# A fused convolution and MLP kernel: a reworked prologue (w1 centred by 32-row matmuls, one load queue, idle matmuls) and fewer, larger token groups

## The chip, the cores and the metric

The kernel runs on 1 core of one Trainium2 chip. The metric is device time in microseconds (us) of the whole program; lower is better. Faster or slower needs 2%.

The engines have their names from the profile: PE multiplies matrices (PEld is its weight load), DVE, ACT and POOL work on vectors, SP issues DMA transfers. The granted clock is the share of its full clock that PE had by the profile; "half clock" means that it reads 0.50.

## The reference, cut to what matters

```python
# x: (8, 4224, 192) f32, weight: (8 heads, 7 taps)
w = softmax(weight)                                   # over the taps
y[b, s, h, :] = sum_k w[h, k] * x_padded[b, s + k, h, :]   # causal, 24 channels a head
# then, on y:
xn = (y - mean) / sqrt(var + 1e-6) * g_ln
out = y + relu(xn @ w_ch1) @ w_ch2                    # w_ch1 192x768, w_ch2 768x192, both given as float64
```

## The kernel before

Each of the 128 partitions holds 33 consecutive tokens of a sequence. A group is n tokens of each partition, 128 n tokens in all. For every group DVE convolves (7 taps x 8 heads = 56 instructions), transposes in 32x32 blocks and takes statistics; PE multiplies by w1 in 32-row tiles ("up"), ACT applies the ReLU, PE multiplies by w2 with the full array ("down"), DVE scales and adds. The mean is not subtracted from the tokens: w1 is centred instead, once, in the prologue. The weights arrive as float64 and are unpacked by integer and float instructions on DVE and ACT. Up, in before:

```python
for f in range(NF):                       # 6 slices of 128 hidden channels
    ph = [psum.tile([P, 512], F32, tag="ps") for q in range(NQ)]      # 4 of the 8 banks
    for c in range(NC):                   # 6 x 32 input channels
        for q in range(NQ):               # 4 row tiles, concurrent: a "quad"
            rows = slice(C * q, C * q + C)
            nc.tensor.matmul(ph[q][:, 0 : n * C], w1[rows, c, fs], t[rows, 0:n, c, :], ...)
    for q in range(NQ):
        nc.scalar.activation(ht[g][:, f, 0:n, q, :], ph[q]..., AF.Relu)
```

Down takes a bank for two tokens, from the same eight; DVE's add frees it. The order in which the engines get their work:

```python
first_tap(0); conv(0); centre_w1(); first_tap(1); transpose(0)
# unpack w2
for g in range(NG):
    load_x(g + 2)
    if g == 0: conv(1)
    up(g)
    if g > 0: first_tap(g + 1); conv(g + 1)
    transpose(g + 1)
    stats(g)
    down(g)            # matmuls on PE, then the adds on DVE, then the store
```

So on DVE the adds of group g come after the convolution, the transpose and the statistics that stand ahead of them.

## Time and profile before

| | before |
|---|---|
| median of its first 3 runs (range) | 1081.69 us (1080.77 to 1082.42) |
| profiled span | 1080.5 us |
| PE starts group 0 | 37.7 us |
| one group of 11 tokens on PE | 43.2 us |
| sequence 0 on PE (7, 8, 9, 9 tokens) | 132.0 us, of it about 2 waiting |

PE is busy from 37.7 us to the last microseconds. The work behind that cannot shrink, so read the table as: what comes ahead of 37.7, what PE loses between pieces of work, and where it waits. The lines themselves stand in the prediction.

### The profile page before, as it was taken

The numbers are of one execution on the slowest core, as the hardware profiler recorded it, in microseconds if no ns is written. First come the engines' busy times: TensorE is split into PE (matmuls) and PEld (weight loads), VectorE is DVE, ScalarE is ACT, GpSimd is POOL, SyncE is SP. The second block draws the span as 40 slices with busy tenths as digits, with TensorE's granted clock in tenths as the row PEclk, the third lists the DMA queues.
The fourth block names the chain that finished last, engine by engine and source line by source line (L and its number), as shares of the span: only waits on it lengthen the run. The fifth ranks groups of instructions, "written<-read, shape, count | busy, mean of one in ns | idle before, by whom it ended". The sixth has DMA issues, their size and how long they took to land.

```text
span 1080.5 us, 24335 instructions
## 1 busy us (share of the span) xinstructions
PE 1057.4 (98%) x10512; PEld 898.8 (83%) x10512; DVE 822.2 (76%) x2363; ACT 240.3 (22%) x636; POOL 16.9 (2%) x23
## 2 busy tenths in 40 slices
PE   3999999999999999999999999999999999999998
PEld 3999987978978879789788797897887978978878
DVE  5999798696696876966968769669687696696821
ACT  3521122031131220311312203113122031131220
POOL 3000000000000000000000000000000000000000
PEclk9999999999999999999999999999999999999999
DMA  8022022022022020230220302203202022020011
GB/s 241 2 82 89 4 96 96 30 75 103 2 103 89 16 104 31 74 103 1 104 102 3 103 31 74 104 1 103 102 2 103 32 73 104 1 104 41 2 42 41
DMA packets 9195, 70.55 MB, mean 65 GB/s; under 512 B 1280, under 2 KB 2304, under 8 KB 3329
## 3 DMA queue, kind: packets, MB, share of 16 engines
q1 hardware_dynamic: 8768, 68.02, 18.3%
q8 instruction: 82, 1.34, 0.5%
q10 hardware_dynamic: 224, 0.98, 0.4%
q14 instruction: 25, 0.20, 0.1%
q0 software_dynamic: 96, 0.00, 0.0%
HBM read 43.05 MB, written 25.95 MB: 64 GB/s over the span
## 4 chain that ended last, share of the span: by engine, by line
PE 96%; DVE 2%; DMA 1%; issue 0%; ACT 0%; ACTq 0%; DVEq 0%
PE po L352 48%; PE ph L329 48%; DVE y L265 1%; DMA raw<-in_moe_w_ch_dram 1%; DVE yt L273 0%; DVE w1f L184 0%; DVE scale1a L174 0%; ACT scale1b L166 0%; DVE scale1b L174 0%; DVE power1a L163 0%; DVE mant1a L157 0%; DVE power1a L159 0%; DVE y L357 0%; ACTq L130 0%; DVE power1b L163 0%
## 5 line engine op out<-in xcount | busy, mean ns | idle before, releaser
L352 PEld LDWEIGHTS po<-w,ht 128*128 128x128 f32 x3168 | 513.5, 190 | 13.3 <-issue 11.7
L352 PE MATMUL po<-w,ht 128*128 128x192 f32 x3168 | 522.5, 327 | 0.0
L329 PE MATMUL ph<-yt,w 32*128 32x352 f32 (+3 forms) x7200 | 520.4, 444 | 1.0 <-DVE yt L273 1.0
L329 PEld LDWEIGHTS ph<-yt,w 32*128 32x128 f32 x7200 | 367.4, 185 | 146.1 <-issue 5.4
L265 DVE SCALAR_TENSOR_TENSOR y<-xg,taps,y 128x264 f32<-128x264 f32 (+3 forms) x1200 | 473.7, 474 | 0.0
L334 ACT ACTIVATE ht<-ph 128x352 f32<-128x352 f32 (+3 forms) x600 | 222.7, 459 | 792.3 <-PE ph L329 792.3
L357 DVE SCALAR_TENSOR_TENSOR y<-po,r,y 128x192 f32<-128x192 f32 x264 | 96.5, 412 | 228.0 <-PE po L352 225.3
L286 DVE BATCH_NORM_STATS2 st<-y 128x6 f32<-128x192 f32 x264 | 70.1, 341 | 0.0
L273 DVE STREAM_TRANSPOSE yt<-y 128x2112 f32<-128x2112 f32 (+3 forms) x25 | 57.3, 2290 | 0.9
L257 DVE TENSOR_SCALAR y<-xg,taps 128x264 f32<-128x264 f32 (+1 forms) x184 | 51.4, 351 | 0.0
L237 PE MATMUL pw<-w1f,centre 128*128 128x128 f32 x144 | 18.0, 292 | 18.7 <-DVE w1f L184 18.7
L237 PEld LDWEIGHTS pw<-w1f,centre 128*128 128x128 f32 x144 | 17.9, 208 | 18.6 <-issue 18.6
L101 POOL MEMSET xg<- 1x1152 f32 x8 | 8.4, 1048 | 779.6 <-DVE y L265 779.6
L312 DVE SCALAR_TENSOR_TENSOR r<-d,r 128x11 f32<-128x11 f32 (+3 forms) x75 | 12.7, 170 | 2.6
L308 DVE TENSOR_TENSOR d<-r 128x11 f32<-128x11 f32 (+3 forms) x75 | 12.7, 170 | 2.6
L309 DVE SCALAR_TENSOR_TENSOR d<-d,v 128x11 f32<-128x11 f32 (+3 forms) x75 | 12.7, 170 | 2.6
L240 ACT COPY w<-pw 128x512 f32<-128x512 f32 (+1 forms) x12 | 5.7, 477 | 8.8 <-PE pw L237 8.6
L255 ACT ACTIVATE y<-xg,taps 128x168 f32<-128x168 f32 (+1 forms) x16 | 5.6, 432 | 0.0
L157 DVE TENSOR_SCALAR mant1a<-raw 128x768 uint32<-128x768 uint32 x1 | 0.6, 559 | 6.0 <-DMA raw<-in_moe_w_ch_dram 6.0
L289 DVE TENSOR_TENSOR d<-st 128x11 f32<-128x11 f32 (+3 forms) x25 | 4.4, 177 | 0.9
L300 DVE TENSOR_SCALAR d<-v 128x11 uint32<-128x11 uint32 (+3 forms) x25 | 4.3, 173 | 0.9
L297 DVE TENSOR_SCALAR v<-v 128x11 f32<-128x11 f32 (+3 forms) x25 | 4.3, 173 | 0.9
(46 smaller groups left out, 47.4 us busy)
## 6 DMA issues: line engine op xcount, KB each, us to landing
xg<-in_x_dram SPq DMA_DIRECT2D x14, 1632.0 KB, 9.2
out_dram<-y SPq DMA_DIRECT2D x20, 1056.0 KB, 4.9
xg<-in_x_dram SPq DMA_DIRECT2D x7, 1428.0 KB, 10.8
xg<-in_x_dram SPq DMA_DIRECT2D x2, 1440.0 KB, 12.5
out_dram<-y SPq DMA_DIRECT2D x2, 864.0 KB, 4.4
xg<-in_x_dram SPq DMA_DIRECT2D x1, 1344.0 KB, 14.1
xg<-in_x_dram SPq DMA_DIRECT2D x7, 191.2 KB
raw<-in_moe_w_ch_dram SPq DMA_DIRECT2D x1, 1152.0 KB
```

The costliest lines, as they stand in the source:

```text
L237: nc.tensor.matmul(dst, m[:, c, :], w1f[:, s, o : o + P], start=start, stop=not start)
L257: nc.vector.tensor_scalar(out=dst, in0=src, scalar1=tap, scalar2=None, op0=ALU.mult)
L265: nc.vector.scalar_tensor_tensor(out=y[g][:, 0:n, cs], in0=t[:, k : k + n, cs], scalar=taps[:, h, k : k + 1], in1=y[g][:, 0:n, cs], op0=AL ...
L273: nc.vector.transpose(yt[g][:, 0:n].rearrange("p j c t -> p (j c t)"), y[g][:, 0:n].rearrange("p j d -> p (j d)"),)
L286: nc.vector.bn_stats(out=st[:, j, :], in_=y[g][:, j, :])
L308: nc.vector.tensor_tensor(d, r, r, op=ALU.mult)
L309: nc.vector.scalar_tensor_tensor(out=d, in0=d, scalar=-0.5, in1=v, op0=ALU.mult, op1=ALU.mult)
L312: nc.vector.scalar_tensor_tensor(out=r, in0=d, scalar=1.5, in1=r, op0=ALU.add, op1=ALU.mult)
L329: nc.tensor.matmul(ph[q][:, 0 : n * C], w1[rows, c, fs], t[rows, 0:n, c, :], start=(c == 0), stop=(c == NC - 1),)
L334: nc.scalar.activation(ht[g][:, f, 0:n, q, :], ph[q][:, 0 : n * C].rearrange("p (j t) -> p j t", t=C), AF.Relu,)
L352: nc.tensor.matmul(dst, t[:, f, j, :, :].rearrange("p q t -> p (q t)"), w2[:, f, :], start=(f == 0), stop=(f == NF - 1),)
L357: nc.vector.scalar_tensor_tensor(out=yg[:, j, :], in0=dst, scalar=rstd[g][:, j : j + 1], in1=yg[:, j, :], op0=ALU.mult, op1=ALU.add,)
```

## The change

The intent: let PE start sooner (w1's bytes first, w1 unpacked in an order that needs less of it at once, centring by a copy and a subtraction of the mean in 32-row tiles, a first group of 6 tokens), keep PE's clock up until it starts (24 idle matmuls), and have fewer group borders (16 and 17 tokens a group in place of 11, each up in two halves so that a matmul still fits a bank). The setup tensors share the room of the later hidden tile, and x has two buffers in place of three. The loads of x0 (the tokens of group 0) are cut differently too, their padding apart from the tokens; that part is not in this core of the diff:

```diff
-        sizes = [J] * (R // J) + [R % J] * (R % J > 0)
-        if b == 0:
-            rest = R - 15
-            sizes = [7, 8, rest // 2, rest - rest // 2]
+        for n in (6, 8, 10, R - 24) if b == 0 else (J - 1, J):      # J = 17, R = 33
 ...
-    xpool = ctx.enter_context(tc.tile_pool(name="xin", bufs=3))
+    xpool = ctx.enter_context(tc.tile_pool(name="xin", bufs=2))
 ...
-    nc.gpsimd.dma_start(out=ga, in_=g_col[0:P, :])
+    nc.scalar.dma_start(out=ga, in_=g_col[0:P, :])
 ...
-    nc.scalar.dma_start(
-        out=raw1[:, 1:3].rearrange("p s f w -> p (s f w)"), in_=w1_words[0:P, :]
+    nc.sync.dma_start(
+        out=raw1[:, 0:2].rearrange("p s f w -> p (s f w)"), in_=w1_words[0:P, :]
     )
     for r in range(2):
-        (nc.sync, nc.scalar)[r].dma_start(
-            out=raw1[Q * r : Q * r + Q, 0, :, :].rearrange("p f w -> p (f w)"),
+        nc.sync.dma_start(
+            out=raw1[Q * r : Q * r + Q, 2, :, :].rearrange("p f w -> p (f w)"),
 ...
     def centre_w1():
-        (72 products of 128x128 with centre = 1 - 1/D, 12 copies)
+        for r in range(2):                          # the means, on all partitions
+            nc.tensor.matmul(pm[:, 0:FH], share[0], w1f[:, r, :], start=True, stop=False)
+            nc.tensor.matmul(pm[:, 0:FH], share[1 + r], w1f[:, 2, :], start=False, stop=True)
+            nc.scalar.copy(mean[:, FH * r : FH * r + FH], pm[:, 0:FH])
+        for s, parts in (...):                      # copy 32 rows to 128, take the mean off
+            ... nc.tensor.matmul(pw[q][:, 0:FH], copy[rows], w1f[rows, s, :], ...)
+            ... nc.tensor.matmul(pw[q][:, 0:FH], less[rows], mean[rows, ...], ...)
+            ... nc.scalar.copy(w1[:, c, FH * r : FH * r + FH], pw[q][:, 0:FH])
+    def keep_warm(times):
+        idle = psum.tile([P, 512], F32, tag="ps", name="idle")
+        for _ in range(times):
+            nc.tensor.matmul(idle[:, 0:P], less, copy, start=True, stop=True)
 ...
+        half = n if n <= 11 else (n + 1) // 2
         for f in range(NF):
+            for i0 in range(0, n, half):            # a block: 6 quads into 4 banks
 ...
     centre_w1()
+    keep_warm(24)
     first_tap(1)
```

Note the third index of raw1: in before slot 0 holds the two 192 KB transfers with the last 64 rows of w1 and slots 1 and 2 the 768 KB transfer; in the changed kernel the 768 KB come first.

More of the change, by code (lines that the diff above doesn't have):

```diff
@@ L51 @@
     R = S // P
-    J = 11
+    J = 17
     NF = F // P
@@ L56 @@
     FH = F // 2
-    assert D == P + Q and S % P == 0 and J * C <= 512 and NF % 2 == 0
+    assert D == P + Q and S % P == 0 and R % 2 and R // 2 + 1 == J and NF % 2 == 0
     groups = []
     for b in range(B):
-        sizes = [J] * (R // J) + [R % J] * (R % J > 0)
-        if b == 0:
-            rest = R - 15
-            sizes = [7, 8, rest // 2, rest - rest // 2]
         j0 = 0
-        for n in sizes:
+        for n in (6, 8, 10, R - 24) if b == 0 else (J - 1, J):
             groups.append((b, j0, n))
             j0 += n
-        assert j0 == R and max(sizes) <= J
+        assert j0 == R
+    assert max(n for _, _, n in groups) <= J
     NG = len(groups)
@@ L100, in load_x @@
             return
+        if b:
+            nc.sync.dma_start(
+                out=flat[:, 0 : (PAD + n) * D],
+                in_=bass.AP(
+                    tensor=x.tensor, offset=(b * S - PAD) * D, ap=[[R * D, P], [1, (PAD + n) * D]]
+                ),
+            )
+            nc.gpsimd.memset(t[0:1, 0:PAD, :], 0.0)
+            return
         nc.gpsimd.memset(t[0:1, 0:PAD, :], 0.0)
+        nc.sync.dma_start(out=flat[:, PAD * D : (PAD + n) * D], in_=xr[b, :, 0 : n * D])
         for p0, p1 in ((16, P), (1, 16)):
             nc.sync.dma_start(
-                out=flat[p0:p1, 0 : (PAD + n) * D],
-                in_=bass.AP(
-                    tensor=x.tensor, offset=(b * S + p0 * R - PAD) * D,
-                    ap=[[R * D, p1 - p0], [1, (PAD + n) * D]],
-                ),
+                out=flat[p0:p1, 0 : PAD * D],
+                in_=xr[b, p0 - 1 : p1 - 1, (R - PAD) * D : R * D],
             )
-        nc.sync.dma_start(out=flat[0:1, PAD * D : (PAD + n) * D], in_=xr[b, 0:1, 0 : n * D])
     taps = consts.tile([P, H, K], F32, name="taps")
@@ L117, with carve @@
     gb = consts.tile([P, 1], F32, name="gb")
-    raw1 = setup.tile([P, 3, FH, 2], U32, name="raw1")
+    room = hpool.tile([P, NF * J * P], F32, tag="ht", name="room")
+    taken = [0]
+    def carve(n, dtype):
+        part = room[:, taken[0] : taken[0] + n].bitcast(dtype)
+        taken[0] += n
+        return part
+    raw1 = carve(6 * FH, U32).rearrange("p (s f w) -> p s f w", f=FH, w=2)
     raw2 = setup.tile([P, NF * D, 2], U32, name="raw2")
@@ L122 @@
     g_col = moe_g_ln.rearrange("(d o) -> d o", o=1)
-    nc.gpsimd.dma_start(out=ga, in_=g_col[0:P, :])
+    nc.scalar.dma_start(out=ga, in_=g_col[0:P, :])
     for r in range(2):
-        nc.gpsimd.dma_start(out=gb[Q * r : Q * r + Q, :], in_=g_col[P:D, :])
+        nc.scalar.dma_start(out=gb[Q * r : Q * r + Q, :], in_=g_col[P:D, :])
     nc.sync.dma_start(
@@ L129 @@
     )
-    nc.scalar.dma_start(
-        out=raw1[:, 1:3].rearrange("p s f w -> p (s f w)"), in_=w1_words[0:P, :]
+    nc.sync.dma_start(
+        out=raw1[:, 0:2].rearrange("p s f w -> p (s f w)"), in_=w1_words[0:P, :]
     )
     for r in range(2):
-        (nc.sync, nc.scalar)[r].dma_start(
-            out=raw1[Q * r : Q * r + Q, 0, :, :].rearrange("p f w -> p (f w)"),
+        nc.sync.dma_start(
+            out=raw1[Q * r : Q * r + Q, 2, :, :].rearrange("p f w -> p (f w)"),
             in_=w1_words[P:D, 2 * FH * r : 2 * FH * (r + 1)],
@@ L148, with split_words @@
     nc.vector.memset(low, -896.0 * (1 << 23))
-    def split_words(raw, name):
-        n = raw.shape[1]
+    def split_words(raw, mant, power):
         hi = raw[:, :, 1]
-        mant = setup.tile([P, n], I32, name="mant" + name)
-        power = setup.tile([P, n], I32, name="power" + name)
-        high = setup.tile([P, n], F32, name="high" + name)
-        scale = setup.tile([P, n], I32, name="scale" + name)
         nc.vector.tensor_single_scalar(mant.bitcast(U32), hi, 0xFFFFF, op=ALU.bitwise_and)
-        nc.scalar.activation(high, mant, AF.Relu, scale=2.0**-20, bias=1.0)
+        nc.scalar.activation(mant.bitcast(F32), mant, AF.Relu, scale=2.0**-20, bias=1.0)
         nc.vector.tensor_scalar(
@@ L165, in split_words, with join_words @@
         )
-        nc.scalar.activation(scale, power, AF.Relu, scale=float(1 << 23), bias=low)
-        return high, scale
-    def join_words(dst, raw, high, scale, gain=None):
+        nc.scalar.activation(power, power, AF.Relu, scale=float(1 << 23), bias=low)
+    def join_words(dst, raw, mant, power, g=None):
         lo, hi = raw[:, :, 0], raw[:, :, 1]
+        mant, power = mant.bitcast(F32), power.bitcast(U32)
         nc.vector.scalar_tensor_tensor(
-            out=high, in0=lo, scalar=2.0**-52, in1=high, op0=ALU.mult, op1=ALU.add
+            out=mant, in0=lo, scalar=2.0**-52, in1=mant, op0=ALU.mult, op1=ALU.add
         )
         nc.vector.scalar_tensor_tensor(
-            out=scale.bitcast(U32), in0=hi, scalar=0x80000000, in1=scale.bitcast(U32),
+            out=power, in0=hi, scalar=0x80000000, in1=power,
             op0=ALU.bitwise_and, op1=ALU.bitwise_or,
         )
-        if gain is None:
-            nc.vector.tensor_tensor(dst, high, scale.bitcast(F32), op=ALU.mult)
+        power = power.bitcast(F32)
+        if g is None:
+            nc.vector.tensor_tensor(dst, mant, power, op=ALU.mult)
             return
-        n = dst.shape[1] // len(gain)
-        for i, g in enumerate(gain):
-            part = slice(n * i, n * i + n)
-            nc.vector.scalar_tensor_tensor(
-                out=dst[:, part], in0=high[:, part], scalar=g, in1=scale.bitcast(F32)[:, part],
-                op0=ALU.mult, op1=ALU.mult,
-            )
-    w1f = setup.tile([P, 3, FH], F32, name="w1f")
+        nc.vector.scalar_tensor_tensor(
+            out=dst, in0=mant, scalar=g, in1=power, op0=ALU.mult, op1=ALU.mult
+        )
+    w1f = carve(3 * FH, F32).rearrange("p (s f) -> p s f", f=FH)
     raw1a = raw1[:, 0:2].rearrange("p s f w -> p (s f) w")
@@ L199 @@
     nc.scalar.activation(taps, taps, AF.Exp)
-    parts_a = split_words(raw1a, "1a")
     nc.vector.tensor_reduce(wsum, taps, axis=AX.X, op=ALU.add)
@@ L206 @@
     )
-    join_words(w1f[:, 0:2].rearrange("p s f -> p (s f)"), raw1a, *parts_a, (gb, ga))
-    parts_b = split_words(raw1b, "1b")
-    join_words(w1f[:, 2], raw1b, *parts_b, (ga,))
+    words_a = (raw1a, carve(2 * FH, I32), carve(2 * FH, I32))
+    words_b = (raw1b, carve(FH, I32), carve(FH, I32))
+    split_words(*words_a)
+    join_words(w1f[:, 0:2].rearrange("p s f -> p (s f)"), *words_a, ga)
+    split_words(*words_b)
+    join_words(w1f[:, 2], *words_b, gb)
     w1 = consts.tile([P, NC, F], F32, name="w1")
@@ L216 @@
     w2 = w2flat.rearrange("p (c d) -> p c d", d=D)
-    centre = []
-    for i, (p0, p1, base) in enumerate(((0, P, 0), (0, Q, P), (Q, P, P))):
-        m = setup.tile([P, NC, NQ, C], F32, name=f"centre{i}")
+    copy, less, mean = carve(P, F32), carve(P, F32), carve(F, F32)
+    share = []
+    for p0, p1 in ((0, P), (0, Q), (Q, P)):
+        m = carve(P, F32)
         if p1 - p0 < P:
             nc.gpsimd.memset(m[P - p1 : P - p0], 0.0)
-        nc.gpsimd.memset(m[p0:p1], -1.0 / D)
+        nc.gpsimd.memset(m[p0:p1], 1.0 / D)
+        share.append(m)
@@ L223 @@
+    nc.gpsimd.memset(copy, 0.0)
+    for q in range(NQ):
+        m = copy[C * q : C * q + C].rearrange("p (q i) -> p q i", q=NQ)
         nc.gpsimd.affine_select(
-            out=m[p0:p1], in_=m[p0:p1], pattern=[[-C, NC], [0, NQ], [-1, C]],
-            compare_op=ALU.not_equal, fill=1.0 - 1.0 / D, base=base, channel_multiplier=1,
+            out=m, in_=m, pattern=[[0, NQ], [-1, C]],
+            compare_op=ALU.not_equal, fill=1.0, base=0, channel_multiplier=1,
         )
-        centre.append(m.rearrange("p c q i -> p c (q i)"))
+    nc.gpsimd.memset(less, -1.0 / C)
@@ L229, in centre_w1 @@
     def centre_w1():
-        for f in range(NF):
-            r, o = divmod(f * P, FH)
-            for c0, c1 in ((0, 4), (4, NC)):
-                pw = psum.tile([P, 512], F32, tag="ps", name=f"pw{f}_{c0}")
-                for c in range(c0, c1):
-                    dst = pw[:, (c - c0) * P : (c - c0 + 1) * P]
-                    for m, s, start in ((centre[0], 1 + r, True), (centre[1 + r], 0, False)):
-                        nc.tensor.matmul(
-                            dst, m[:, c, :], w1f[:, s, o : o + P], start=start, stop=not start
-                        )
-                nc.scalar.copy(
-                    w1[:, c0:c1, f * P : f * P + P],
-                    pw[:, 0 : (c1 - c0) * P].rearrange("p (c f) -> p c f", f=P),
-                )
+        for r in range(2):
+            pm = psum.tile([P, 512], F32, tag="ps", name=f"pm{r}")
+            nc.tensor.matmul(pm[:, 0:FH], share[0], w1f[:, r, :], start=True, stop=False)
+            nc.tensor.matmul(pm[:, 0:FH], share[1 + r], w1f[:, 2, :], start=False, stop=True)
+            nc.scalar.copy(mean[:, FH * r : FH * r + FH], pm[:, 0:FH])
@@ new lines, in centre_w1 @@
+        for s, parts in (
+            (0, [(q, 0) for q in range(NQ)]),
+            (2, [(NQ, 0), (NQ + 1, 0), (NQ, 1), (NQ + 1, 1)]),
+            (1, [(q, 1) for q in range(NQ)]),
+        ):
+            pw = [psum.tile([P, 512], F32, tag="ps", name=f"pw{s}_{q}") for q in range(NQ)]
+            for q in range(NQ):
+                rows = slice(C * q, C * q + C)
+                nc.tensor.matmul(
+                    pw[q][:, 0:FH], copy[rows], w1f[rows, s, :], start=True, stop=False
+                )
+            for q, (c, r) in enumerate(parts):
+                rows = slice(C * q, C * q + C)
+                nc.tensor.matmul(
+                    pw[q][:, 0:FH], less[rows], mean[rows, FH * r : FH * r + FH],
+                    start=False, stop=True,
+                )
+            for q, (c, r) in enumerate(parts):
+                nc.scalar.copy(w1[:, c, FH * r : FH * r + FH], pw[q][:, 0:FH])
@@ L322, in up @@
         ht[g] = hpool.tile([P, NF, J, NQ, C], F32, tag="ht", name=f"ht{g}")
+        half = n if n <= 11 else (n + 1) // 2
         for f in range(NF):
             fs = slice(f * P, f * P + P)
-            ph = [psum.tile([P, 512], F32, tag="ps", name=f"ph{g}_{f}_{q}") for q in range(NQ)]
-            for c in range(NC):
+            for i0 in range(0, n, half):
+                js = slice(i0, min(i0 + half, n))
+                w = (js.stop - js.start) * C
+                ph = [
+                    psum.tile([P, 512], F32, tag="ps", name=f"ph{g}_{f}_{i0}_{q}")
+                    for q in range(NQ)
+                ]
+                for c in range(NC):
+                    for q in range(NQ):
+                        rows = slice(C * q, C * q + C)
+                        nc.tensor.matmul(
+                            ph[q][:, 0:w], w1[rows, c, fs], t[rows, js, c, :],
+                            start=(c == 0), stop=(c == NC - 1),
+                        )
                 for q in range(NQ):
-                    rows = slice(C * q, C * q + C)
-                    nc.tensor.matmul(
-                        ph[q][:, 0 : n * C], w1[rows, c, fs], t[rows, 0:n, c, :],
-                        start=(c == 0), stop=(c == NC - 1),
-                    )
-            for q in range(NQ):
-                nc.scalar.activation(
-                    ht[g][:, f, 0:n, q, :],
-                    ph[q][:, 0 : n * C].rearrange("p (j t) -> p j t", t=C), AF.Relu,
-                )
+                    nc.scalar.activation(
+                        ht[g][:, f, js, q, :],
+                        ph[q][:, 0:w].rearrange("p (j t) -> p j t", t=C), AF.Relu,
+                    )
     def down(g):
@@ L342, in down @@
         yg = y.pop(g)
-        ends = (n,) if g + 1 < NG else (4, 8, 10, n)
+        ends = (n,) if g + 1 < NG else (4, 8, 12, 14, 16, n)
         done = 0
@@ L372 @@
     centre_w1()
+    keep_warm(24)
     first_tap(1)
     transpose(0)
-    parts = split_words(raw2, "2")
-    join_words(w2flat, raw2, *parts)
+    words_2 = (
+        raw2, setup.tile([P, NF * D], I32, name="mant"), setup.tile([P, NF * D], I32, name="power")
+    )
+    split_words(*words_2)
+    join_words(w2flat, *words_2)
     for g in range(NG):
```

## The prediction

> **What bounds the kernel now.** I read the page first (busy time by engine, the 40 slices), then the chain that ended last, then the timeline of the first 75 us, of the small groups and of one large group, then the waits. PE is the bound: it is busy 98% of the span, and every slice but the first reads 9.
>
> ```profile
> PE 1057.4 (98%) x10512; PEld 898.8 (83%) x10512; DVE 822.2 (76%) x2363; ACT 240.3 (22%) x636; POOL 16.9 (2%) x23
> PE   3999999999999999999999999999999999999998
> ```
>
> PE's real work cannot shrink: the change keeps every product of the two large layers. So three things can move the time: when PE starts group 0, what PE loses at group and block borders, and where it waits. The start, from the timeline (start, duration, engine, line, operation, count; in brackets the idle time before and what ended it):
>
> ```profile
> 13.16 0.56 DVE L157 TENSOR_SCALAR mant1a<-raw 128x768 uint32<-128x768 uint32 x1 [6.00 <-DMA raw<-in_moe_w_ch_dram]
> 18.66 18.02 PE L237 MATMUL pw<-w1f,centre 128*128 128x128 f32 x144 [18.66 <-DVE w1f L184]
> 21.27 14.69 DVE L265 SCALAR_TENSOR_TENSOR y<-xg,taps,y 128x168 f32<-128x168 f32 x48
> 35.99 1.58 DVE L273 STREAM_TRANSPOSE yt<-y 128x1344 f32<-128x1344 f32 x1
> 37.71 14.71 PE L329 MATMUL ph<-yt,w 32*128 32x224 f32 x288 [1.02 <-DVE yt L273]
> ```
>
> Read it upwards: PE starts group 0 at 37.71, released by the transpose, which follows the convolution of 7 tokens (14.69), which follows the unpacking of w1 (13.16 to 21.27), which waited for w1's bytes. Centring w1 (18.66 to 36.7) lies beside the convolution and ends 1.0 us before PE is needed: nearly a tie, so a faster convolution alone would gain only 1 us; both must shrink, and the change shrinks both.
>
> Steady groups of 11 have no wait: up starts at 169.72, down at 191.23, the next up at 212.93, the one after at 256.13. A group costs 43.2 us. The small second group has a wait:
>
> ```profile
> 66.20 16.95 PE L329 MATMUL ph<-yt,w 32*128 32x256 f32 x288
> 67.52 2.37 DVE L357 SCALAR_TENSOR_TENSOR y<-po,r,y 128x192 f32<-128x192 f32 x7
> 69.15 1.22 ACT L334 ACTIVATE ht<-ph 128x256 f32<-128x256 f32 x4 [15.94 <-PE ph L329]
> 69.61 13.14 PEld L329 LDWEIGHTS ph<-yt,w 32*128 32x128 f32 x236 [0.36 <-DVE y L357]
> 72.42 1.21 ACT L334 ACTIVATE ht<-ph 128x256 f32<-128x256 f32 x4 [2.05 <-PE ph L329]
> 75.01 1.21 ACT L334 ACTIVATE ht<-ph 128x256 f32<-128x256 f32 x4 [1.38 <-PE ph L329]
> 77.60 1.21 ACT L334 ACTIVATE ht<-ph 128x256 f32<-128x256 f32 x4 [1.38 <-PE ph L329]
> ```
>
> One block (6 quads of 8-token matmuls) takes 2.59 us (72.42 to 75.01 to 77.60), but the first spacing is 3.27: the second block needs banks that the previous group's down results hold until DVE has added them (67.52 to 69.89). The wait is 0.7 us there, 1.1 over the whole up (16.88 against 6 x 2.59 + 0.2).
>
> **What the Trainium skill says.** "TensorEngine Tiling (Array Packing)", Key Properties: changing the tiling mode drains TensorE. Up runs in 32-row tiles and down in 128x128, so each group has two switches. The trace agrees: 11-token blocks are 3.55 apart, 6 x 3.55 = 21.30, but up to down is 21.51, so a switch costs 0.2 us. "TensorE: Matmul & The Clock Gate", Part 1: PE runs at half clock after an idle window of about 3.4 us and needs as long to return. The trace agrees: the first centring matmuls take 550 ns, the median 275. This is what the idle matmuls are for. "DMA: Bandwidth & Descriptors", Issuing engines are not separate DMA queues: queues of different issuers share the 16 engines and interleave. The trace agrees: w1's last 192 KB on ACT's queue took 11.8 us to land beside x0 on SP's queue.
>
> **The change part by part.**
>
> *Start.* With one queue w1 (1152 KB) goes before x0 (6 tokens and 6 of padding, 1152 KB; before 1243). The two-us windows of the start show 0.14 MB moved by 4 us, 0.75 by 6, 1.15 by 8, 1.50 by 10, 1.98 by 12, 2.38 by 14. At that rate w1's first 768 KB are through at about 6.3 us and all of it at 8.3, x0 at 14. With 1.5 to 2 us for the last packet and the receipt (my choice; taps alone took 5.9) w1's first part lands near 8.5 (before: all of it at 13.06), x0 near 16. DVE's unpacking took 8.1 us (13.16 to 21.27). The tap sums (0.6) now come ahead, so 7.6: ready at 8.6 + 7.6 = 16.2. ACT's first taps wait for x0 at 16, the convolution 0.4 behind: it starts at 16.5, both inputs nearly tied. An instruction of it costs 306 ns at 168 elements (14.69/48), 331 at 192 and 356 at 216, that is 1.04 ns an element; at 144 elements 281, x 48 = 13.5 us. The transpose is 1.58 - 0.2 = 1.4. Start of PE: 16.5 + 13.5 + 1.4 + 0.1 = 31.5, **6.2 us earlier**. Is w1 centred by then? In place of 72 products of 128x128 (18.0 us) there are 4 for the means and 6 quads of 384 columns, each 0.64 us (128 columns take 0.223 as ACT's copies, 2.68 us per 12, show): 6.4 us, some 8 with the cold clock. ACT's 14 copies of about 0.45 us, behind its first taps, end near 27, the 24 idle matmuls (24 x 0.223 = 5.4) near 30. Off the path, by little.
>
> *Borders.* n = 11: 43.2 us x 3 = 129.6 us per sequence of 33. New: 16 tokens are 12 blocks x 2.59 = 31.1, down 96 x 0.325 (12 matmul passes per 3.90 us pair) = 31.2, switches 0.4: 62.7. 17 tokens: 6 x (2.59 + 2.91) = 33.0, down 33.15, 0.4: 66.55. Sum 129.25. The extra blocks cost 5 ns a quad, the saved switch 0.4 us. **Seven sequences: -2.45 us.**
>
> *Sequence 0.* Before: 37.71 to 169.72 = 132.0 us. New, without waits: n = 6: 23.8, 8: 31.5, 10: 39.3, 9: 35.4, sum 130.0. The waits, with T the start of PE:
> - Up(0): its first ReLU stands on ACT behind the two passes over w2 (as at 41.97 before). 0.6.
> - DVE after transpose(0): w2 unpacking 7.4, convolution(1) 15.9, transpose 1.75 = 25.0, as from 37.57 to 62.59 before. PE, with 6 tokens where it had 7, is done at T + 24.4 (before it came 3.6 later than the transpose). Wait 0.6.
> - Then PE runs ahead of DVE: the second block of up(1) wants three banks at T + 27.6, and DVE frees them only after statistics(0) (6 x 0.27 + 3.1 = 4.7) and the adds (0.34 each): T + 30.3, 31.0, 31.7. Wait 4.0, where it was 1.1.
> - Up(4), n = 16, after a group of 9: DVE has first taps and convolution of 16 tokens (8 x 0.33 + 48 x 0.531 = 28.1), transpose 3.4, statistics 5.5 and an add 0.7 = 37.7 from T + 100.3, so the bank comes at T + 138.05; PE wants it at T + 135.3. Wait 2.8.
> Sum 8.0 against 2.0 before: sequence 0 lasts 138.0, **+6.0**.
>
> Later groups: DVE needs 29.4 + 3.6 + 7.6 + 5.7 = 46 us for 17 tokens, PE 66.5; no wait. Two x buffers suffice: convolution(g) has freed its buffer before the load of g + 2 is issued, and that has a whole group (over 60 us) to land in, against 9 us for 1632 KB. The end is unchanged: one token, one small store, 3.4 us after PE.
>
> Sum: 1081.7 - 6.2 - 2.45 + 6.0 = 1079.1; I say 1079.3.
>
> **Rivals.** (1) The start gains little because x0, not w1, sets it: before, x0's last rows landed at 18.1 (issued 2.6, 15.5 to landing). If they do again, the convolution starts at 18.5 and the time is 1081. For it: the first 17 us move only some 200 GB/s, though the engines are fully busy, then 440. Against: x0 is smaller and nothing interleaves with it. If the full rate came at once, the unpacking alone would bound, PE would start near 29.5, and the time would be 1077. (2) The waits are worse: in the 4 us of up(1) PE is nearly idle, the clock may fall, and the next 3.4 us run at half speed, +2 us: 1081. Or they are not there, because DVE gains elsewhere: 1072. I see nothing that shortens DVE's 25.0. (3) Blocks of 8 are bound by weight loads: 16.88/36 = 469 ns a quad in the 8-token group against 440 assumed here with the switch; 21 such blocks a run x 36 x 0.03 = 23 us, 1102. Against: its steady spacing is 2.59 and 7 tokens reach 2.27, both 5 ns a quad above 53.3 ns a token. (4) DVE becomes the bound in the large groups: against it 46 to 66.5.
>
> **Range and chances.** The start is uncertain by 2 us, the waits by 3, the borders by 1. I take 1075 to 1084.5. Two per cent is 21.6 us, which only (3) would reach: slower 0.02, faster 0.02, within 0.96.
>
> **What would show it.** Right: up(0) starts at 30 to 33; 8-token blocks 2.59 apart; a second block of up(1) that waits some 4 us for DVE's adds and a first block of up(4) that waits some 3; no PE wait from group 5 on; 129.25 us a sequence. Wrong: w1 landing after 11 us, idle matmuls running into up(0), a block spacing over 2.65, a DMA releasing a convolution after group 1, or first matmuls of a group at twice their length.

## The result, and the profile after

| | before | changed |
|---|---|---|
| median (6 runs each) | 1081.59 us (1080.57 to 1082.42) | 1080.01 us (1078.99 to 1080.94) |
| ratio of fast runs | | 0.9986, 95% interval 0.9973 to 0.9999 |
| profiled span, mean granted clock | 1080.5 us, 1.00 | 1078.5 us, 0.997 |

A ratio here is the mean time of one kernel's fast runs over that of the other's of the same rounds, so it is not quite the ratio of the medians quoted. The change is worth 1.6 us: the same, by the 2% rule. The predicted 1079.3 was 0.7 us off, inside the range of 1075 to 1084.5. But the trace shows that two terms of the sum were off by more, in opposite directions.

The page of the changed kernel, the lines that answer to the first of before:

```profile
PE 1057.6 (98%) x12488; PEld 997.0 (92%) x12488; DVE 753.5 (70%) x1851; ACT 255.4 (24%) x806; POOL 11.1 (1%) x23
PE   4999999999999999999999999999999999999998
```

DVE has 512 instructions and 69 us less to do (fewer groups), and that bought nothing: PE is the bound and is as busy as before. The start, from the timeline (columns as in the prediction's):

```profile
7.49 0.56 DVE L165 TENSOR_SCALAR room<-room 128x768 uint32<-128x768 uint32 x1 [0.91 <-DMA room<-in_moe_w_ch_dram]
14.87 13.48 DVE L294 SCALAR_TENSOR_TENSOR y<-xg,taps,y 128x144 f32<-128x144 f32 x48
21.22 4.69 ACT L266 COPY w<-pw 128x384 f32<-128x384 f32 x12 [1.43 <-PE pw L261]
24.39 5.62 PE L272 MATMUL idle<-room 128*128 128x128 f32 x48
28.39 1.38 DVE L302 STREAM_TRANSPOSE yt<-y 128x1152 f32<-128x1152 f32 x1
29.94 12.22 PE L366 MATMUL ph<-yt,w 32*128 32x192 f32 x288
```

The unpacking starts at 7.5 us (13.2 before), the convolution at 14.9 (21.3), PE on group 0 at 29.94: 7.8 us earlier, where 6.2 was predicted. The centring's copies end at 25.9, the transpose at 29.8 and the idle matmuls at 30.0: the last two are a near tie.

The waits of PE, from the same timeline:

```profile
53.99 3.28 PE L366 MATMUL ph<-yt,w 32*128 32x256 f32 x50
58.24 2.04 DVE L394 SCALAR_TENSOR_TENSOR y<-po,r,y 128x192 f32<-128x192 f32 x6
59.04 13.20 PE L366 MATMUL ph<-yt,w 32*128 32x256 f32 x188 [1.77 <-DVE y L394]
75.17 15.87 PE L389 MATMUL po<-w,ht 128*128 128x192 f32 x96
165.68 0.71 PE L366 MATMUL ph<-yt,w 32*128 32x256 f32 x6
168.07 3.02 DVE L394 SCALAR_TENSOR_TENSOR y<-po,r,y 128x192 f32<-128x192 f32 x9
168.87 33.03 PE L366 MATMUL ph<-yt,w 32*128 32x256 f32 x570 [2.48 <-DVE y L394]
201.83 31.47 PE L389 MATMUL po<-w,ht 128*128 128x192 f32 x192
```

Up(1) runs from 53.99 to 75.17, 21.2 us, and should take 6 x 2.59 + 0.2 = 15.7: 5.4 us lost. Its second block stands still until DVE, at 58.24, begins the adds of group 0 that free the banks. Up(4), the first of 16 tokens, runs from 165.68 to 201.83, 36.15 us, where later groups of 16 take 31.3: 4.9 us lost, for the same reason. The windows of time say why each loss is larger than the wait (columns: window, its length, then for PE, its weight loads, DVE, ACT and POOL the busy time with the number of instructions; then the granted clock, DMA share, GB/s):

```profile
57.00:60.00 3.00, 1.23 (x5) 0.59 (x4) 2.72 (x12) 1.15 (x4) 0.00 (x0) 1.00 0.00 0
60.00:63.00 3.00, 3.00 (x34) 2.39 (x36) 3.00 (x12) 0.00 (x0) 0.00 (x0) 0.68 0.79 250
63.00:66.00 3.00, 3.00 (x48) 2.74 (x44) 3.00 (x9) 1.21 (x4) 0.00 (x0) 0.76 0.87 338
66.00:70.00 4.00, 4.00 (x80) 3.79 (x78) 4.00 (x12) 1.53 (x6) 0.00 (x0) 1.00 0.20 81
169.00:172.00 3.00, 3.00 (x44) 2.72 (x48) 3.00 (x10) 0.00 (x0) 0.00 (x0) 0.71 0.05 19
172.00:176.00 4.00, 4.00 (x64) 3.67 (x60) 4.00 (x11) 1.60 (x6) 0.00 (x0) 0.79 1.02 344
```

While PE waits (57 to 60) the clock is still full. Just when it has work again (60 to 66, 169 to 176) the clock is lowered: 3 x 0.32 + 3 x 0.24 = 1.7 us of full clock are missing at the first place and 3 x 0.29 + 4 x 0.21 = 1.7 at the second. From group 5 on there is no wait: a sequence takes 31.29 + 31.40 + 33.21 + 33.35 = 129.25 us, exactly the predicted sum.

The balance from the two traces: start -7.8, sequence 0 with the loss at up(4) 140.6 against 132.0, so +8.6, seven sequences -2.45; sum -1.65 us. Spans differ by 2.0, medians by 1.6.

### The profile page after: what moved, and what is told of

Its sections match the earlier page's. It is cut to its first block, busy times and chain, and to the rows that moved or that the text cites. A ratio compares the mean times of both kernels' runs of the same rounds, so it can differ in the third digit from the quotient of the medians.

```text
span 1078.5 us, 27860 instructions
## 1 busy us (share of the span) xinstructions
PE 1057.6 (98%) x12488; PEld 997.0 (92%) x12488; DVE 753.5 (70%) x1851; ACT 255.4 (24%) x806; POOL 11.1 (1%) x23
## 4 chain that ended last, share of the span: by engine, by line
PE 91%; DVE 8%; DMA 1%; issue 0%; ACT 0%; SPq 0%; DVEq 0%
PE ph L366 45%; PE po L389 45%; DVE y L294 5%; DVE yt L302 1%; DMA room<-in_moe_w_ch_dram 1%; DVE st L315 0%; DVE y L286 0%; DVE y L394 0%; ACT room L174 0%; DVE room L182 0%; DVE power L182 0%; DVE w L188 0%; ACT power L174 0%; DVE d L338 0%; DVE r L341 0%
## 5 line engine op out<-in xcount | busy, mean ns | idle before, releaser
L366 PE MATMUL ph<-yt,w 32*128 32x256 f32 (+3 forms) x9216 | 524.0, 383 | 4.3 <-DVE y L394 4.3
L366 PEld LDWEIGHTS ph<-yt,w 32*128 32x128 f32 x9216 | 471.6, 186 | 53.3 <-DVE y L394 5.8
L294 DVE SCALAR_TENSOR_TENSOR y<-xg,taps,y 128x384 f32<-128x384 f32 (+5 forms) x864 | 429.8, 578 | 0.0
L371 ACT ACTIVATE ht<-ph 128x256 f32<-128x256 f32 (+3 forms) x768 | 237.8, 396 | 772.3 <-PE ph L366 772.3
L302 DVE STREAM_TRANSPOSE yt<-y 128x3072 f32<-128x3072 f32 (+5 forms) x18 | 56.0, 3112 | 0.6
L286 DVE TENSOR_SCALAR y<-xg,taps 128x408 f32<-128x408 f32 (+3 forms) x128 | 43.1, 410 | 0.0
L244 PE MATMUL pm<-room 128*128 128x384 f32 x4 | 3.1, 880 | 12.3 <-DVE room L190 12.3
L337 DVE TENSOR_TENSOR d<-r 128x16 f32<-128x16 f32 (+5 forms) x54 | 9.4, 175 | 1.9
L341 DVE SCALAR_TENSOR_TENSOR r<-d,r 128x16 f32<-128x16 f32 (+5 forms) x54 | 9.4, 175 | 1.9
L338 DVE SCALAR_TENSOR_TENSOR d<-d,v 128x16 f32<-128x16 f32 (+5 forms) x54 | 9.4, 174 | 1.9
L245 PE MATMUL pm<-room 128*128 128x384 f32 x4 | 3.1, 880 | 1.2 <-DVE room L190 1.2
```

What stands on the lines that cost most here:

```text
L286: nc.vector.tensor_scalar(out=dst, in0=src, scalar1=tap, scalar2=None, op0=ALU.mult)
L294: nc.vector.scalar_tensor_tensor(out=y[g][:, 0:n, cs], in0=t[:, k : k + n, cs], scalar=taps[:, h, k : k + 1], in1=y[g][:, 0:n, cs], op0=AL ...
L302: nc.vector.transpose(yt[g][:, 0:n].rearrange("p j c t -> p (j c t)"), y[g][:, 0:n].rearrange("p j d -> p (j d)"),)
L337: nc.vector.tensor_tensor(d, r, r, op=ALU.mult)
L338: nc.vector.scalar_tensor_tensor(out=d, in0=d, scalar=-0.5, in1=v, op0=ALU.mult, op1=ALU.mult)
L341: nc.vector.scalar_tensor_tensor(out=r, in0=d, scalar=1.5, in1=r, op0=ALU.add, op1=ALU.mult)
```

## The experiments

The theory after the result (A): the prologue is worth its 7.8 us, the larger groups 2.45, and the sizes 6, 8, 10, 9 give most of it back in two waits for DVE's adds, each followed by half clock. Rivals: the start was not worth that much because DVE bounds sequence 0 whatever the sizes (B), and others named below. Eleven kernels ran, all with correct results, in three batches; before ran in the rounds of each (medians 1081.72, 1081.72 and 1081.39). The batches (E1 to E4, E5 to E8, E9 to E11) ran on three chips; where a run is compared with one of another batch, the medians of before say how far that can be trusted.

| run | edit | median us (runs) | ratio to before, 95% |
|---|---|---|---|
| E1 | change, sizes of before | 1075.79 (5) | 0.9949, 0.9936 to 0.9961 |
| E2 | change, 7, 7, 9, 10 | 1071.23 (4) | 0.9905, 0.9890 to 0.9920 |
| E3 | change, 6, 8, 9, 10 | 1075.87 (5) | 0.9948, 0.9935 to 0.9960 |
| E4 | change, idle matmuls in both waits | 1077.05 (5) | 0.9959, 0.9946 to 0.9971 |
| E5 | E2 without the 24 idle matmuls | 1074.34 (5, one slow) | 0.9931, 0.9917 to 0.9945 |
| E6 | change without the 24 idle matmuls | 1077.63 (5) | 0.9969, 0.9956 to 0.9981 |
| E7 | E2 with the queues of before | 1072.85 (4) | 0.9919, 0.9905 to 0.9932 |
| E8 | before with one queue | 1080.57 (5) | 0.9986, 0.9972 to 1.0000 |
| E9 | E1 with the old centring, no idle matmuls | 1079.95 (5) | 0.9988, 0.9975 to 1.0000 |
| E10 | change, 6, 7, 9, 11 | 1073.12 (5) | 0.9927, 0.9913 to 0.9940 |
| E11 | change, 7, 7, 8, 11 | 1071.81 (4) | 0.9913, 0.9900 to 0.9927 |

### E1 to E3: the sizes alone

```diff
-        for n in (6, 8, 10, R - 24) if b == 0 else (J - 1, J):
+        for n in (7, 8, 9, R - 24) if b == 0 else (11, 11, 11):     # E1
+        for n in (7, 7, 9, R - 23) if b == 0 else (J - 1, J):       # E2
+        for n in (6, 8, 9, R - 23) if b == 0 else (J - 1, J):       # E3
```

> All of the change but the group sizes, which are those of before (7, 8, 9, 9, then 11, 11, 11). Theory A (the early start is worth its full 7.8 us less one token's convolution, and the new sizes give most of it back in two waits for DVE's adds, with half clock after each): PE starts at 31.3, 6.4 us earlier than before, up(1) waits about 1.1 us as before, no half-clock window; PE loses 7 x 0.35 us in the large groups against the change. 1074 us, 6 us under the changed kernel and 7.5 under before. Rival B (the start was never worth that much, because DVE in sequence 0 is the bound whatever the sizes): 1080 to 1081, as the changed kernel.

Measured 1075.79, 5.9 us under before. All of the change but its sizes is worth nearly four times what the change is worth with them. PE starts at 32.3 in this trace, as w1 landed 1 us later than in the other runs; up(1) takes 16.5 us, and the granted clock reads 1.00 until PE's last work. (The column also reads 1.00 over the first centring matmuls of before, which take 550 ns where the median is 275, so it says nothing of the first microseconds.) B falls.

> Only the sizes of sequence 0, 7, 7, 9, 10 in place of 6, 8, 10, 9. Theory A: group 0 gives PE 3.9 us more work and DVE 1.0 us less before it has to free the banks, and a group of 10 ahead of the first 16 gives PE 39.3 us where DVE needs 37.7; so both waits go (5.4 and 4.9 us with their half clock), the start is 1.35 us later: 1071 us, no half-clock window before the end. Rival B (waits only move to other groups): 1078 or more, with the same idle time of PE elsewhere.

Measured 1071.23: the expectation to 0.2 us, 8.8 us under the changed kernel's 1080.01 and 10.5 under before of the same rounds. From its timeline:

```profile
53.44 1.88 DVE L315 BATCH_NORM_STATS2 st<-y 128x6 f32<-128x192 f32 x7
58.45 2.37 DVE L394 SCALAR_TENSOR_TENSOR y<-po,r,y 128x192 f32<-128x192 f32 x7
58.94 7.28 PE L366 MATMUL ph<-yt,w 32*128 32x224 f32 x148
161.33 3.95 PE L366 MATMUL ph<-yt,w 32*128 32x256 f32 x68
```

DVE begins the adds of group 0 (58.45) before PE begins up(1) (58.94), so the banks are free when the second block needs them: up(1) takes 13.8 us, as 6 x 2.27 + 0.2 says, and up(4), from 161.33, the 31.3 of the later groups of 16. One token more in group 0 costs 1.3 us of start (31.26 for 29.94) and gives PE 3.9 us of work that DVE uses to catch up. The waits do not move elsewhere.

> Only the order of 10 and 9 exchanged: 6, 8, 9, 10. Theory A: the wait at group 4 (4.9 us with its half clock) goes, that at group 1 (5.4) stays: 1075.2 us, one half-clock window near 61 us. Rival B: the wait moves to group 3 or stays, 1080.

Measured 1075.87. Exchanging 10 and 9 alone takes 4.1 us off: up(4) is 31.3 us, up(1) still 21.1 with its half clock. So the two losses are separate, and each is where the trace of the changed kernel has it.

### E4: is the clock part of the loss?

```diff
+                if (g, f, i0) in ((1, 1, 0), (4, 0, 0)):
+                    for _ in range(10):
+                        nc.tensor.matmul(
+                            ph[0][:, 384:512], w1[:, 0, 0:P], w2flat[:, 0:P], start=True, stop=True
+                        )
                 for c in range(NC):
```

> Ten idle matmuls of 128 columns (about 2.2 us) ahead of the second block of up(1) and of the first of up(4), into unused columns of a bank that is free, so that PE is not idle while it waits for DVE. Theory A (each wait costs a half-clock window of 3.4 us on top, 1.7 us of work): granted clock 1.00, up(1) 19.5 in place of 21.2 us, up(4) 34.4 in place of 36.15, time 1076.7. Rival C (the half clock falls where PE would wait anyway, or the window is there with the idle matmuls too): 1080, no change; the waits alone make up the whole loss.

Measured 1077.05, 3.0 us less, with more work on PE and not one wait shortened. The windows (columns as above):

```profile
57.00:60.00 3.00, 3.00 (x29) 2.79 (x26) 2.69 (x12) 1.21 (x4) 0.00 (x0) 1.00 0.00 0
60.00:63.00 3.00, 3.00 (x52) 2.52 (x53) 3.00 (x12) 0.12 (x1) 0.00 (x0) 1.00 0.70 231
166.00:169.00 3.00, 2.74 (x42) 2.14 (x44) 2.85 (x10) 0.00 (x0) 0.00 (x0) 1.00 0.01 3
```

PE is kept busy from 57 to 60, and the clock is 1.00 from 60 to 63, where the changed kernel had 0.68. Up(1) is 19.3 us (21.2), up(4) 34.6 (36.15). So of the 10.3 us lost in the two places about 3 are clock, the rest is the waiting itself. An idle matmul in a wait is a repair; E2 removes the wait.

### E5 and E6: the 24 idle matmuls ahead of group 0

```diff
-    keep_warm(24)
```

> Sizes 7, 7, 9, 10 without the 24 idle matmuls ahead of group 0. PE is then idle from about 24.4 to 31.3. Theory A (the idle matmuls save half a half-clock window, and in this version nothing behind them hides it): up(0) begins at half clock, 1.7 us longer (15.5 for 13.8), time 1072.9 against 1071.2 with them. Rival D (idle matmuls do nothing, as the window of the clock ends before up(0) or lies otherwise): 1071.2.

Measured 1074.34, with 1073.75 to 1074.70 in its four fast runs: 3.1 us more than E2, twice what was expected. D falls for this version.

> The changed kernel, sizes 6, 8, 10, 9, without the 24 idle matmuls. Theory A: up(0) is 1.7 us longer at half clock, but up(1) waits for DVE's adds anyway, so its wait is 1.7 us shorter: 1080.0, no change, or up to 1.7 us less if the shorter wait no longer brings a half-clock window. Rival D: if the loss is on the path in spite of the wait, 1081.7.

Measured 1077.63: 2.4 us *less* than the changed kernel. This went further than the expectation. The windows around the start of group 0 show how costly the missing idle matmuls are there:

```profile
24.00:28.00 4.00, 0.25 (x1) 0.00 (x0) 4.00 (x15) 4.00 (x13) 0.00 (x0) 0.76 0.00 0
28.00:32.00 4.00, 1.78 (x23) 1.81 (x27) 3.93 (x7) 1.58 (x3) 0.00 (x0) 0.50 0.59 181
32.00:36.00 4.00, 4.00 (x56) 4.00 (x55) 3.91 (x4) 2.26 (x5) 0.00 (x0) 0.50 0.53 216
36.00:40.00 4.00, 4.00 (x103) 4.00 (x100) 4.00 (x13) 1.65 (x8) 0.00 (x0) 0.96 0.02 6
```

The clock is at half before group 0 begins at 30.2 and stays there to 36, some 6 us of work, so up(0) takes 14.9 us in place of 12.15: 2.75 lost, not 1.7. E5's 3.1 us, where nothing hides it, fits that; its fast runs have the same mean clock, 0.995, but no trace shows it. In E6 it is hidden: up(1) then starts 3.0 us later, DVE is nearly done with its adds, up(1) takes 16.8 us in place of 21.2, and no half clock follows. The rest, 1.7 us, is at up(4): there it waits as before (34.5 us), but in this execution without half clock. The two idle times are equally long, 2.48 us in the changed kernel and 2.49 here, so their length did not decide:

```profile
167.50 31.34 PE L366 MATMUL ph<-yt,w 32*128 32x256 f32 x570 [2.49 <-DVE y L394]
```

In windows of 0.1 us the half clock lasts 3.41 us each time in the changed kernel, E3, E10 and E11, and 10.24 us, three times that, from 26.10 in E6; the two of the changed kernel begin at 61.06 and 170.28, which is 32 x 3.41 apart. An estimate from these figures: the clock is set anew every 3.41 us, by what PE did in the 3.41 us before. Counted so, the changed kernel's idle time at up(4) lay with 2.0 us in one such span, E6's with about 1.0 and 1.5 us in two. That fits, but no run was made to test it.

By the medians, the same idle matmuls gain 3.1 us at the sizes 7, 7, 9, 10 and lose 2.4 at 6, 8, 10, 9: what the path does later decides. The second figure is the weaker one: of E6's five runs three took 1077.3 to 1077.6 and two 1079.8, which is the expectation's "no change".

### E7 to E9: what moved the start

```diff
-    nc.sync.dma_start(out=raw1[:, 0:2]..., in_=w1_words[0:P, :])    # E7, from E2; ga, gb to gpsimd
+    nc.scalar.dma_start(out=raw1[:, 0:2]..., in_=w1_words[0:P, :])
-        nc.sync.dma_start(out=raw1[Q * r : Q * r + Q, 2, :, :]...
+        (nc.sync, nc.scalar)[r].dma_start(out=raw1[Q * r : Q * r + Q, 2, :, :]...
```

> Sizes 7, 7, 9, 10 with the loads of w1 and of the gains on the queues that before had (ACT and SP, GpSimd), all else as changed. Theory A (w1 behind x0 in shared engines is what held the start): the unpacking begins at 13.2 in place of 7.4, PE starts 5.7 us later, 1076.9. Rival E (the order of the queues matters little; new centring and sizes give the start): 1071.5 to 1073.

Measured 1072.85, 1.6 us more than E2, not 5.7: the order of the queues is worth little in this version. The lines that show it, E7's start of the unpacking and of group 0:

```profile
8.56 0.56 DVE L165 TENSOR_SCALAR room<-room 128x768 uint32<-128x768 uint32 x1
15.28 2.71 ACT L284 ACTIVATE y<-xg,taps 128x168 f32<-128x168 f32 x8 [0.50 <-DMA xg<-in_x_dram]
32.39 13.90 PE L366 MATMUL ph<-yt,w 32*128 32x224 f32 x288 [1.36 <-DVE yt L302]
```

With both queues the unpacking begins at 8.56, 1.1 us after E2's 7.43 and 4.6 before the 13.16 of before. The largest difference to before that the traces show is what the first pass needs. There it takes the two 192 KB transfers (slot 0) and half of the 768 KB one. The DMA issues of before show that the 768 KB had landed 8.7 us after their issue at 0.76, at 9.5 us, while the last 192 KB landed 11.8 us after 1.20, at 13.0; unpacking began at 13.16:

```profile
raw<-in_moe_w_ch_dram ACTq DMA_DIRECT2D x1, 768.0 KB, 8.7
raw<-in_moe_w_ch_dram ACTq DMA_DIRECT2D x1, 192.0 KB, 11.8
```

In the changed kernel the first pass needs the 768 KB alone. My theory had named one line of the diff and missed this one. It is not the whole difference either: in E7 the later of the two 192 KB transfers landed at 11.2 us (10.0 after 1.20), not at 13.0, so with the old order of slots the unpacking would have begun about 1.9 us earlier than in before all the same. The loads of x0 are cut differently there, and no run takes that part by itself.

> The kernel before with nothing but the w1 loads moved to SP's queue ahead of x0, and the gains to ACT's. Theory A: unpacking begins near 7.5, the convolution (7 tokens) at 15.6 and ends near 30.3; but the old centring (18 us, from 13 to 31, and its last copies) now ends together with the transpose: PE starts near 32.4, 5.3 us earlier than before, 1076.4; the new centring alone would be worth about 1 us. Rival E: 1081, as before.

Measured 1080.57, 1.1 us less than before, not 5.3.

```profile
10.41 0.56 DVE L157 TENSOR_SCALAR mant1a<-raw 128x768 uint32<-128x768 uint32 x1 [4.17 <-DMA raw<-in_moe_w_ch_dram]
34.97 4.82 PE L329 MATMUL ph<-yt,w 32*128 32x224 f32 x96 [0.38 <-DVE yt L273]
```

With the old order of slots the first pass waits for all three transfers and begins at 10.41, so the convolution begins at 18.5 and the transpose ends at 34.8; the old centring, which also starts only when w1 is unpacked (15.92 to 34.6), and its last copy end at 35.0, together with it. PE starts at 35.0, 2.7 us earlier than before, and loses 0.65 of that in up(0), 15.3 us for 14.65. So by itself the order of the queues brings the unpacking forward by 2.75 us (13.16 to 10.41), more than the 1.1 it was worth between E7 and E2, where the other parts were in place: the parts overlap, and their shares depend on the order in which they are taken.

```diff
-        (new centring)                          # E9, from E1
+        (72 products of before, with w1f slots 0, 1 and 2)
-    keep_warm(24)
```

> Sizes of before (7, 8, 9, 9, 11s) and all of the change's loads and unpacking, but the centring of before (72 products of 128x128, no idle matmuls). Theory F (what moved the start is that the first two thirds of the unpacking no longer need the 192 KB halves of w1, and the new centring is what lets PE use it): unpacked at 14.9, the old centring takes 18.7 us, PE starts group 0 at about 34.2 instead of 32.3 in the run of the same sizes, and ACT, which copies until then, delays up(0) by 0.8: 1078.6 against 1075.8. Rival G (the centring was beside other work and stays so): 1075.8.

Measured 1079.95, 4.2 us more than E1: the expectation was 2.8, in the right direction. Its timeline:

```profile
16.19 18.05 PE L244 MATMUL pw<-room,centre 128*128 128x128 f32 x142 [2.06 <-DVE room L190]
30.68 1.58 DVE L280 STREAM_TRANSPOSE yt<-y 128x1344 f32<-128x1344 f32 x1
34.17 4.82 PE L344 MATMUL ph<-yt,w 32*128 32x224 f32 x96
39.91 10.07 PE L344 MATMUL ph<-yt,w 32*128 32x224 f32 x192 [0.91 <-ACT ht L349]
```

The transpose is done at 32.3, but PE is centring until 34.2: what was beside the path is now on it. PE starts 1.9 us later than E1, and because ACT copies for the centring until then, its other work comes late: up(0) waits 0.9 us for a ReLU at 39.91 and takes 15.7 us in place of 13.8, and group 1 starts 3.8 us later than in E1. So the new order of the slots gains little while the old centring stands; the new centring with the old order of slots was not run.

### E10 and E11: other sizes

```diff
+        for n in (6, 7, 9, R - 22) if b == 0 else (J - 1, J):       # E10
+        for n in (7, 7, 8, R - 22) if b == 0 else (J - 1, J):       # E11
```

> Sizes 6, 7, 9, 11, with the early start of a first group of 6. Worked out as the waits were: DVE frees the banks for the second block of up(1) 2.6 us late, with a half-clock window 4.3 us; none at group 4. 1074.5, 3 us behind 7, 7, 9, 10 in spite of the start 1.35 us earlier; without a half-clock window 1072.8. Rival (an earlier start is always worth it): 1070.

Measured 1073.12, and the single runs match both numbers expected: the two with mean clock 0.998 took 1074.7 us, the three with 1.00 took 1072.7 to 1073.1. The profiled execution is one of the former; its up(1) takes 18.2 us in place of 13.8. An earlier start with a wait behind it loses to a later one without: 1.9 us behind E2.

> Sizes 7, 7, 8, 11: the wait of 0.3 us that 7, 7, 9, 10 was worked out to have at up(2) goes. 1070.9, not to be told from 1071.2; no wait of PE for DVE's adds.

Measured 1071.81, not to be told from E2 by the intervals. No wait for adds, as expected; but E2's trace had none at up(2) either (17.7 us, as for 9 tokens elsewhere), so there was nothing to gain. The profiled execution, alone of the four (mean clock 0.998, the others 1.00), has a half clock that was not expected: in it group 0 starts at 31.12, 2.0 us after the last idle matmul, the clock is 0.79 from 31 to 33 and 0.50 from 33 to 35, and up(0) takes 15.5 us in place of 13.8.

```profile
31.12 15.59 PE L366 MATMUL ph<-yt,w 32*128 32x224 f32 x288 [1.96 <-DVE yt L302]
```

In E2, with 1.3 us between them, it is 1.00 throughout.

**The version that beats both kernels** is E2: 1071.23 us, a ratio of 0.9905 to before (0.9890 to 0.9920). That is clear of noise, and still "the same" by the 2% rule.

## Why the prediction was right

Point by point, by its own steps:

- **PE's work cannot shrink, the change moves only the start, the borders and the waits.** Right: PE's busy time is 1057.4 before and 1057.6 after. (A slip of reading: of the 40 slices the last reads 8, not 9.)
- **Start, -6.2.** Right in direction, 1.6 us too small. The unpacking began at 7.49, not 8.6; x0 was not tied with it (ACT's first taps followed its last unpacking at 13.62 without a wait for DMA), so the convolution began at 14.87, not 16.5. Convolution 13.5, transpose 1.4: as measured, 13.48 and 1.38. The cause given was only a part. The unpacking begins 5.7 us earlier, and "With one queue w1 (1152 KB) goes before x0" is worth 1.1 us of that when the rest is in place (E7) and 2.75 by itself (E8). The rest is that the first pass no longer reads slot 0's late transfers and that these landed earlier, perhaps by the new cut of x0's loads; no run separates the two. The prediction compared w1's "first part" with "all of it at 13.06" without saying that it was the order of the slots that let the first part be used.
- **Centring off the path by little.** Right: copies end at 25.9 (27 predicted), idle matmuls at 30.0 (30), PE starts at 29.94. E9 shows that without it 4.2 us are lost.
- **Borders, -2.45.** Right to the hundredth: 129.25 us a sequence.
- **Waits of sequence 0, +6.0.** This was +8.6. By terms: up(0) 12.15 us, so 0.25 lost where 0.6 was said. DVE's 25.0 us from transpose to transpose were 23.8, because unpacking w2 took 6.2 us (29.70 to 35.87), not 7.4: ACT, no longer copying for the centring, answers at once (in before DVE stood 1.28 us for it there). So the wait of 0.6 ahead of up(1) is gone. Up(1) lost 5.4 where 4.0 was said, up(4) 4.9 where 2.8 was said; about 3.4 of these 10.3 is half clock. Without it the two waits are 3.7 and 3.2, close to what was worked out. The term of the sum that was mis-sized is thus the half clock, which the prediction had only as rival (2), for one of the two places, with 2 us.
- **Rivals.** (1) fell in its first half, a late x0; its second half, a start near 29.5 with the time at 1077, is what came for the start. (2) came true, twice: E4 gets 3.0 us back by keeping PE busy. (3) fell: blocks of 8 are 2.59 apart everywhere. (4) fell: DVE is busy 70% and nothing waits for it from group 5 on.

So the number was right because the main waits were seen and sized from the trace of before, and because two errors, a start 1.6 us too late and 2.6 us of waits too few, partly cancelled. That they did is luck.

## What to carry to other kernels

Before moving a start forward, work out for each engine when it will be done with the *next* group and who frees the banks it needs: here one token more in the first group (1.3 us of start) was worth 8.8 us together with one more at group 3, because DVE then kept ahead of PE. Waits of 3.2 and 3.7 us on PE cost half as much again (1.7 us each) in granted clock here, so look at the clock of the windows behind each wait. And ask of a load not when all of it lands but which piece the first instruction reads.

## What the Trainium skill lacked or had wrong

- "TensorE: Matmul & The Clock Gate", table "Why this matters for your kernels", advises no PE-idle gaps over about 3 us between bursts. That is too long: a gap of 1.96 us was followed by half clock in E11's profiled execution, one of 1.3 us was not in E2; one of 2.48 us at up(4) was followed by it in the changed kernel, one of 2.49 was not in E6. The page's Part 1 does say that its window is free-running, and the traces agree (stretches of 3.41 us, two of them begun 109.2 us = 32 x 3.41 apart). What it lacks is how much idle time within one window is enough: by the count under E6, 1.5 us was not and 1.85 us was (PE idle from 24.25, half clock from 26.10), both estimates from these traces.
- "TensorEngine Tiling (Array Packing)", Key Properties, says that a mode switch drains TensorE but gives no cost: 0.2 us a switch here, between 32-row tiles and the full array in float32.
- "DMA: Bandwidth & Descriptors" does not say that transfers at the start of a program can be slow: before moved 206 GB/s from 6 to 13 us and 229 from 13 to 18, with the engines busy all the time, and 435 from 18 to 24. E2, with its loads in one queue, moved 288 from 6 to 13 and 396 from 13 to 18. The packets differ too (of before's 599 from 13 to 18 us 567 are under 2 KB, of the 460 from 18 to 24 255), but from 6 to 13 us only 134 of 355 are, at 206 GB/s. What causes it stays open.
